# A banded attention with a feed-forward block: another weighing in the scheduler that writes out its order

## The chip, the cores and the metric

The kernel runs on one core of a Trainium2 chip. The metric is the device time of one execution in microseconds (us), taken as the median of three runs. Engines are named as in the profile: PE is TensorE (matrix products), DVE is VectorE, ACT is ScalarE, POOL is GpSimd, and SP is the engine whose queue issues nearly all DMAs.

## The reference

Attention over 4 batches, 8 heads, 768 positions and 64 columns a head, in which a position sees the last `n_local` positions and the first `n_global`, with a slope per head on the distance; then a layer norm and two matrix products with a ReLU between them, added to the attention's output.

```python
def _attn_ref(q, k, v, n_global, n_local):          # q, k, v: 4 x 8 x 768 x 64
    scores = scale * np.matmul(q, k.transpose(0, 1, 3, 2))
    rel = pos[:, None] - pos[None, :]
    is_global = pos[None, :] < int(n_global)         # 8 here
    is_local = (rel >= 0) & (rel < int(n_local))     # 96 here
    dist = np.where(is_global & ~is_local, float(n_local), np.abs(rel))
    slopes = 2.0 ** (-8.0 * (np.arange(H) + 1) / H)  # 1/2, 1/4, ... 1/256
    scores = np.where(is_global | is_local, scores - slopes * dist, -1e9)
    ...                                              # softmax
    return np.matmul(a, v)

def _moe_ref(x, g_ln, w_ch1, w_ch2):                 # x: 4 x 768 x 512
    xn = (x - mu) / np.sqrt(var + 1e-06) * g_ln
    ch = np.maximum(xn @ w_ch1, 0.0) @ w_ch2         # 512 x 2048 and 2048 x 512, float64
    return x + ch
```

## The kernel before, in words

The work is cut into 24 tiles of 128 positions. Tiles 0 to 3 are the first 128 positions of each batch ("short": one block of keys, computed in fp32); tiles 4 to 23 follow batch by batch and see two blocks of keys. Two tiles make a chunk; the products of the feed-forward block run chunk by chunk. Each value that enters a product in the long part is split in two fp16 numbers, an upper and a lower part, and a product takes three matmuls.

**A short tile t** goes through: load of k, q, v; `tk`, `tq` (PE turns k and q with matmuls against `ident`); `km`, `qm` (ACT or DVE copies them from PSUM to SBUF); `S` (PE, scores in tile `s`); `R` (DVE adds the mask, takes the minimum, into `T`); `E` (ACT, exponential); `tp` (PE turns T), `pl` (copy to `pT`); `P` (PE, `pv`); `X`, `B`, `A`, `C` (DVE: division, statistics, spread, centring to `xs`); `W` (POOL, the root of `rs`); `xr` (scaling of `xs`); `tx` (PE turns it), `xh`, `xl` (ACT upper part and DVE lower part, in `xT`).

**The weights** come as 16 pieces of 1 MB in float64; pieces 0 to 7 are of the first matrix, two pieces for four columns of blocks. Of piece n: `wb` brings it (SP); `wr` (ACT, a relu over the low words); `ws`, the sign step (DVE, one bit of 1024 16-bit words); `wz`, sizes (ACT); `ww`, the shift (DVE); `wu`, the upper half, into `w1h` or `w2h` (ACT, POOL or DVE); `wl`, the lower half, into `w1l` or `w2l` (POOL or DVE). A piece is staged in a tile `st`, or, for six of them, in the later home of other halves, so that it is seen in rows as `w2h` or `w2l`.

**The products.** The first product of chunk c has eight steps, tiles `f_c_0`, `f_c_2`, ... `f_c_14`, of 24 matmuls each. Step f needs `xT` of both tiles of the chunk and pieces 2j and 2j+1 with j = f // 4 rounded down, so f_0_0 and f_0_2 need pieces 0 and 1, f_0_4 and f_0_6 pieces 2 and 3, f_0_8 pieces 4 and 5. ACT and DVE make the two halves of `h` from it, which frees its bank of PSUM. The second product follows two chunks (later one) at a time.

**What sets the order.** Each step is entered as a task with its engines, a cost in us, the tasks that it waits for, the buffers that it takes and a rank. `Plan.order` walks a clock of its own through all tasks: of the tasks that can start next on an engine (within 0.05 us) it takes that with the least rank, and for a task that several engines can do it takes the engine that would end it first. The list that comes out is the order in which each engine gets its instructions, and an engine does them in that order. Tasks marked `port` on DVE, and all on POOL, are never planned at the same time. Where PE is planned to have no work in the first 90 us, `blank` puts matmuls of 512 columns whose result nobody reads. Ranks come from the constants at the head of the file (`QUICK`, `PIECE`, `START`). All instructions are issued through one recording helper, and so all carry line 193 in the profile of before (199 after the change); steps are told apart by their tiles.

Of the kernel before, what the change touches and what calls it, by code (L numbers as in the profile page):

```python
# [16 lines left out]
AF = mybir.ActivationFunctionType  # L17
# [7 lines left out]
P = 128  # L25
# [18 lines left out]
CT = 2  # L44
# [6 lines left out]

QUICK = (0.0, -5.2, 7.7, 16.9)
PIECE = (1.8, 5.3, 15.0)
START = 37.6
SIDE = (-1.1, 1.1)
UNTIL = 90.0
# [28 lines left out]
class Plan:  # L85
# [9 lines left out]
    def order(self):  # L95
# [83 lines left out]
def banded(ctx, tc, q, k, v, n_global, n_local, g_ln, w1, w2, out, flag):  # L179
# [98 lines left out]

    def build_mask0(h, engine):
        if engine == "ACT":  # L280
            act.activation(out=mask0[:, h], in_=made["d0"], func=AF.Copy, scale=Z * 2.0 ** -(h + 1))
        else:
            vec.tensor_scalar_mul(out=mask0[:, h], in0=made["d0"], scalar1=Z * 2.0 ** -(h + 1))

# [3 lines left out]

    def build_mask1(h, engine):
        if engine == "ACT":  # L290
            act.activation(out=mask1[:, h], in_=made["d"], func=AF.Copy, scale=Z * 2.0 ** -(h + 1))
        else:
            (vec if engine == "DVE" else pool).tensor_scalar(out=mask1[:, h], in0=made["d"], scalar1=Z * 2.0 ** -(h + 1), scalar2=None, op0=ALU.mult)

    task("starts", "POOL", 1.0, starts, take={"h": ["mask1_7"]})
    task("warm", "ACT", 1.5, warm, ["ident"], rank=-40)
# [4 lines left out]
    task("distance", "DVE", 1.25, distance, ["away"], rank=-1)  # L301
    for n in range(H):
        h = n % 4 * 2 + n // 4
        task(f"mask0_{h}", {"DVE": 0.17, "ACT": 0.35}, 0, lambda engine, h=h: build_mask0(h, engine), ["distance"], rank=0.1 * n)
    task("globals", "DVE", 0.25, globals_first, [f"mask0_{h}" for h in range(H)], rank=30)
    for h in range(H):
        task(f"mask1_{h}", {"POOL": 0.87, "ACT": 0.42, "DVE": 0.3}, 0, lambda engine, h=h: build_mask1(h, engine), ["globals"], rank=45, port=True)
    task("gb", "SP", 0.6, lambda: load.dma_start(out=gb, in_=g_ln.partition_broadcast(P)), rank=9, dma=0.7)
# [7 lines left out]
    def weight(n):  # L316
# [89 lines left out]
    def quick(t, rank):  # L406
# [107 lines left out]
    def tile_(t, ranks, gates):  # L514
# [91 lines left out]
        else:  # L606
# [21 lines left out]
            kready.append("globals")  # L628
            kready += [f"mask1_{h}" for h in range(H)]

        for g in range(ng_):
            rank = ranks[g]
            slow = 1.05 if short else 0.48
            first_take = {"tile": [f"X{t}"]} if g == 0 else {}
            task(f"S{t}_{g}", "PE", slow, lambda g=g: scores(g), kready + ([f"S{t}_{g - 1}"] if g else []) + gates[g], rank=rank - 20, take={"s": [f"R{t}_{g}"], **first_take})
            task(f"R{t}_{g}", "DVE", 0.85, lambda g=g: reduce(g), [f"S{t}_{g}"] + ([f"mask0_{h}" for h in heads(g)] if short else []), rank=rank - 3, take={"T": [f"tp{t}_{g}" if short else f"pl{t}_{g}"]})
            task(f"E{t}_{g}", "ACT", 1.7 if short else 1.2, lambda g=g: exps(g), [f"R{t}_{g}"], rank=rank - 3)
            if short:
                task(f"tp{t}_{g}", "PE", 0.7, lambda g=g: flip(g), [f"E{t}_{g}"], rank=rank - 20, take={"f1" if t < 2 and g == 0 else "f2": [f"pl{t}_{g}"]}, slack=0.8 * (t > 1))
# [86 lines left out]
    def ffn1(c, f, rank):  # L726
# [353 lines left out]
```

## Time and profile before

| | |
|---|---|
| runs | 628.87 us median of 3, 627.67 to 629.8 |
| profiled execution | 629.0 us, of which 627.1 us span |
| granted clock of PE, mean | 0.989 |
| PE busy | 611.4 us (97%), 5337 matmuls |
| DVE, ACT, POOL busy | 404.2, 329.7, 51.5 us |
| DMA | 88.27 MB, mean 141 GB/s |

The span runs from the first instruction to the last; 1.9 us of the execution lie outside it. Busy time of PE holds the blank matmuls too. A row of the timeline gives start, length, engine, line, operation, tiles written and read, and in brackets how long the engine had been idle before it and what it had waited for. An instruction's length can overlap the next one's start; where spacing matters, starts are compared.

### The profile page before, as it was taken

Reading aid. Unit: us, or ns where it says so; the run is one execution under the profiler, and the core shown is the slowest. Engines: PE = TensorE matmul, PEld = TensorE weight load, DVE = VectorE, ACT = ScalarE, POOL = GpSimd, SP = SyncE. Lnnn points to the kernel's source line nnn. Section 1 sums busy time; section 2 is a strip of 40 time slices with the busy share of each in tenths; the row PEclk is TensorE's granted clock in tenths of the full one; section 3 lists DMA queues with packets and bytes.
Section 4 is the critical chain, followed back from the end, with each engine's and each line's share of the span. In section 5 each row is a group of like instructions: output and inputs, shape, how many; then the busy total and the mean of one; then the engine's idle time right before and its main releaser. Section 6 shows DMA issues by size and latency. Waiting matters only on the chain.

```text
span 627.1 us, 13530 instructions
## 1 busy us (share of the span) xinstructions
PE 611.4 (97%) x5337; PEld 434.5 (69%) x5337; DVE 404.2 (64%) x979; ACT 329.7 (53%) x823; POOL 51.5 (8%) x52
## 2 busy tenths in 40 slices
PE   8979999999999999999999999999999999999995
PEld 4857896457957956956966966965965975975852
DVE  5899999985764763764754754754755744646740
ACT  5888998863644643644644544644652634520200
POOL 2210101130100100110100100200100100000000
PEclk9789999999999999999999999999999999999999
DMA  8982999989758757659657568786577653231000
GB/s 225 322 276 75 240 225 230 219 163 231 149 120 184 103 121 172 108 110 220 109 120 163 112 118 174 132 167 148 114 126 140 126 107 81 56 52 42 10 9 30
DMA packets 247304, 88.27 MB, mean 141 GB/s; under 512 B 237377, under 2 KB 237377, under 8 KB 247233
## 3 DMA queue, kind: packets, MB, share of 16 engines
q1 hardware_dynamic: 246944, 87.32, 65.0%
q8 instruction: 44, 0.72, 0.5%
q14 instruction: 28, 0.22, 0.1%
q10 hardware_dynamic: 288, 0.00, 0.0%
HBM read 38.01 MB, written 6.29 MB: 71 GB/s over the span
## 4 chain that ended last, share of the span: by engine, by line
PE 89%; DVE 6%; DMA 1%; issue 1%; ACT 1%; SPq 0%; DVEq 0%; ACTq 0%
PE f L193 77%; PE s L193 6%; PE pv L193 5%; DVE st L193 1%; DVE w2l L193 1%; DMA w2h<-in_moe_w_ch_dram 1%; DVE T L193 1%; DVE h L193 1%; SPq L193 0%; ACT T L193 0%; DVE w2h L193 0%; DVE xT L193 0%; PE tp L193 0%; PE blank L193 0%; DVE x L193 0%
## 5 line engine op out<-in xcount | busy, mean ns | idle before, releaser
L193 PE MATMUL f<-xT,w1h 128*128 128x256 f16 x1536 | 256.5, 273 | 3.9 <-ACT kT L193 2.2
L193 PE MATMUL f<-w2h,h 128*128 128x512 f16 x768 | 237.2, 379 | 0.3 <-DVE h L193 0.3
L193 PE MATMUL f<-xT,w1l 128*128 128x256 f16 x768 | 210.1, 274 | 0.0
L193 PEld LDWEIGHTS <-h 128*128 128x128 f16 x1152 | 110.1, 98 | 123.9 <-issue 0.6
L193 PEld LDWEIGHTS <-w1h 128*128 128x128 f16 x1536 | 148.2, 98 | 21.6 <-DVE xT L193 2.5
L193 PE MATMUL f<-w2l,h 128*128 128x512 f16 x384 | 145.5, 379 | 0.0
L193 ACT ACTIVATE h<-f 128x512 f16<-128x512 f32 x96 | 56.7, 590 | 91.8 <-PE f L193 91.4
L193 DVE TENSOR_TENSOR pn<-T,pn 128x512 f16<-128x512 f32 x79 | 56.0, 709 | 74.6 <-ACT pn L193 74.6
L193 ACT ACTIVATE T<-T,mn 128x256 f32<-128x256 f32 (+1 forms) x192 | 92.4, 482 | 2.9
L193 DVE SCALAR_TENSOR_TENSOR h<-f,h 128x512 f16<-128x512 f32 x96 | 66.0, 687 | 34.1 <-ACT h L193 34.1
L193 ACT ACTIVATE mn<-nm 128x2 f32<-128x2 f32 (+1 forms) x88 | 17.7, 201 | 124.4 <-DVE nm L193 124.4
L193 PEld LDWEIGHTS <-w1l 128*128 128x128 f16 x768 | 75.3, 98 | 9.7 <-issue 0.8
L193 DVE CUSTOM_DVE_ANT_0 T<-s,mask 128x256 f32<-128x256 f32 (+1 forms) x192 | 68.2, 396 | 11.8 <-PE s L193 10.6
L193 POOL TENSOR_TENSOR rs<-rs,half 128x1 f32<-128x1 f32 x24 | 24.9, 1038 | 429.2 <-DVE rs L193 405.2
L193 PE MATMUL s<-kT,qT 128*128 128x128 f16 (+1 forms) x704 | 55.4, 226 | 1.2 <-ACT T L193 1.2
L193 ACT ACTIVATE pn<-T 128x512 f16<-128x512 f32 x80 | 50.1, 626 | 1.6
L193 PEld LDWEIGHTS <-pT 128*128 128x128 f16 x960 | 38.8, 98 | 10.3
L193 DVE SCALAR_TENSOR_TENSOR x<-f,x 128x512 f32<-128x512 f32 x24 | 16.6, 690 | 40.0 <-PE f L193 40.0
L193 PE MATMUL pv<-vn,pT 128*128 128x64 f16 x960 | 41.0, 193 | 0.0
L193 PEld LDWEIGHTS <-qT 128*128 128x128 f16 x640 | 38.7, 98 | 2.9
L193 ACT ACTIVATION_READ_ACCUMULATOR T<-T,mn 128x1 f32 x192 | 35.9, 187 | 0.0
L193 DVE TENSOR_TENSOR x<-pv,r 128x512 f32<-128x512 f32 x24 | 16.6, 691 | 9.5 <-PE pv L193 8.6
(126 smaller groups left out, 459.4 us busy)
## 6 DMA issues: line engine op xcount, KB each, us to landing
st<-in_moe_w_ch_dram SPq DMA_DIRECT2D x10, 1024.0 KB, 6.1
kf<-in_k_dram SPq DMA_DIRECT2D x28, 256.0 KB, 4.1
vf<-in_v_dram SPq DMA_DIRECT2D x28, 256.0 KB, 3.5
qf<-in_q_dram SPq DMA_DIRECT2D x24, 256.0 KB, 4.1
out_dram<-x SPq DMA_DIRECT2D x24, 256.0 KB, 2.6
qT<-qT SPq DMA_DIRECT2D x40, 128.0 KB, 2.5
w2h<-in_moe_w_ch_dram SPq DMA_DIRECT2D x3, 1024.0 KB, 7.4
w2l<-in_moe_w_ch_dram SPq DMA_DIRECT2D x3, 1024.0 KB, 9.1
```

Source lines behind the costliest of these rows:

```text
L193: ins = getattr(self.engine, name)(*args, **kw)
```

## The change

Four things change. The scheduler, in weighing which engine would end a task first, adds to an engine's time the cost of tasks of that engine alone that stand ready with no higher rank (`behind`). The sign step is entered with 1.33 us instead of 0.7 and is no longer marked `port`. The masks are built by DVE alone, that of one head as half or less of another's, instead of one instruction a head on DVE, ACT or POOL. And more ranks are set apart from each other by a new table, `OFFSET`, with all constants given new values; the weights' loads now come 21 ranks ahead of their work instead of 12.

```diff
-QUICK = (0.0, -5.2, 7.7, 16.9)
-PIECE = (1.8, 5.3, 15.0)
-START = 37.6
-SIDE = (-1.1, 1.1)
+QUICK = (0.0, -3.4, 15.7, 13.1)
+PIECE = (-1.3, 6.5, -36.8)
+START = 30.8
+SIDE = (-0.9, -0.5)
+AHEAD = 0.37
+OFFSET = (2.7, 8.2, -16.5, -0.9, -21.0)
...
+        def behind(engine, key):
+            rank = tasks[key][3]
+            return sum(tasks[k][0][engine] for k, t in ready[engine].items() if len(tasks[k][0]) == 1 and tasks[k][3] <= rank and t < engines[engine] + AHEAD)
...
-                        ends = {o: max(ready[o][key], engines[o]) + c + FAVOR.get(o, 0.0) for o, c in costs.items()}
+                        ends = {o: max(ready[o][key], engines[o] + behind(o, key)) + c + FAVOR.get(o, 0.0) for o, c in costs.items()}
...
-    def build_mask0(h, engine):
...
+    def scaled_down(to, of, power):
+        vec.tensor_scalar_mul(out=to, in0=of, scalar1=2.0 ** -power)
+
+    def build_mask0():
+        vec.tensor_scalar_mul(out=mask0[:, 0], in0=made["d0"], scalar1=Z * 0.5)
+        scaled_down(mask0[:, 2], mask0[:, 0], 2)
+        scaled_down(mask0[:, 4:7:2], mask0[:, 0:3:2], 4)
+
+    def build_odd():
+        scaled_down(mask0[:, 1::2], mask0[:, 0::2], 1)
...
+    def build_mask1():
+        vec.tensor_scalar_mul(out=mask1[:, 0], in0=made["d"], scalar1=Z * 0.5)
+        scaled_down(mask1[:, 1], mask1[:, 0], 1)
+        scaled_down(mask1[:, 2:4], mask1[:, 0:2], 2)
+        scaled_down(mask1[:, 4:8], mask1[:, 0:4], 4)
...
-        task(f"wb{n}", "SP", 0.6, bring, before, rank=rank - 12, take={} if n in homes else {"st": [f"wl{n}"]}, dma=3.0)
+        task(f"wb{n}", "SP", 0.6, bring, before, rank=rank + OFFSET[4], take={} if n in homes else {"st": [f"wl{n}"]}, dma=3.0)
...
-        task(f"ws{n}", "DVE", 0.7, signs, [f"wr{n}"], rank=rank, port=True)
+        task(f"ws{n}", "DVE", 1.33, signs, [f"wr{n}"], rank=rank)
...
-            task(f"E{t}_{g}", "ACT", 1.7 if short else 1.2, lambda g=g: exps(g), [f"R{t}_{g}"], rank=rank - 3)
+            task(f"E{t}_{g}", "ACT", 1.7 if short else 1.2, lambda g=g: exps(g), [f"R{t}_{g}"], rank=rank + (OFFSET[0] if short else -3))
...
-        task(f"hl{c}_{f}", "DVE", 0.7, low, [f"hh{c}_{f}"], rank=rank - 6)
+        task(f"hl{c}_{f}", "DVE", 0.7, low, [f"hh{c}_{f}"], rank=rank + (OFFSET[2] if c < 2 else -6))
```

What this does to the order is seen in three places. SP, at the start of the program, where loads are issued: `kf`, `qf`, `vf` are k, q, v of a short tile, and rows with `in_moe_w_ch_dram` are pieces of weights. Before:

```order
L193 DMA kf_0_99<-in_k_dram 128x8x64
L193 DMA qf_0_111<-in_q_dram 128x8x64
L193 DMA vf_0_114<-in_v_dram 128x8x64
L193 DMA w2h<-in_moe_w_ch_dram 128x2x512
L193 DMA kf_0_131<-in_k_dram 128x8x64
L193 DMA qf_0_154<-in_q_dram 128x8x64
L193 DMA vf_0_164<-in_v_dram 128x8x64
L193 DMA w2h<-in_moe_w_ch_dram 128x2x512
```

The same place of SP after the change:

```order
L199 DMA w2h<-in_moe_w_ch_dram 128x2x512 x2
L199 DMA kf_0_113<-in_k_dram 128x8x64
L199 DMA qf_0_115<-in_q_dram 128x8x64
L199 DMA vf_0_129<-in_v_dram 128x8x64
L199 DMA w2l<-in_moe_w_ch_dram 128x2x512
```

Pieces 0 and 1 have moved ahead of all loads of the first tile. On PE, the first turn of k (`tk`) stood behind 7 blank matmuls and now stands behind 41; before f_0_0 there were 57 blanks in all and 14 later, and now there are 77 and none.

ACT, from its first work on the data on; the rows on `w2h` are steps of pieces 0 and 1, the one on `w1h` is the upper half of piece 0, and `kT`, `qT` are copies of what PE has turned. After the change:

```order
L199 ACTIVATE w2h<-w2h,less 128x1024
L199 ACTIVATE d<-rel,hl 128x256
L199 ACTIVATE w2h,big<-w2h 128x1024
L199 ACTIVATE w2h<-w2h,less 128x1024
L199 ACTIVATE kT_0_194<-tk_186 128x512
L199 ACTIVATE w1h<-w2h 128x2x512
L199 ACTIVATE qT_209<-tq_201 128x512
```

Before, `kT`, `d`, `qT` and four masks came first here and piece 0 followed. Now three weight steps lead, and the copy of the turned k stands between the relu of piece 1 and the upper half of piece 0.

POOL, from its first step after the constants on. Before:

```order
L193 TENSOR_SCALAR mask_88<-d 128x256 x2
L193 TENSOR_TENSOR rs<-rs,half 128x1 x2
L193 TENSOR_TENSOR w1h<-w2l,fill 128x2x512
L193 TENSOR_TENSOR rs<-rs,half 128x1
L193 TENSOR_TENSOR w1l<-st_463,w1h 128x2x512
```

After the change, behind the two halves of piece 2 and two roots, the halves of pieces 3, 4 and 5 and the lower half of piece 7:

```order
L199 TENSOR_TENSOR w1h<-w2l,fill 128x2x512
L199 TENSOR_TENSOR w1l<-w2l,w1h 128x2x512
L199 TENSOR_TENSOR w1h<-st_268,fill 128x2x512
L199 TENSOR_TENSOR w1l<-st_268,w1h 128x2x512
L199 TENSOR_TENSOR w1h<-st_305,fill 128x2x512
L199 TENSOR_TENSOR rs<-rs,half 128x1
L199 TENSOR_TENSOR w1l<-st_305,w1h 128x2x512
L199 TENSOR_TENSOR w1l<-w2h,w1h 128x2x512
```

POOL has 17 steps on weights in all, where it had 2, and 35 lower parts of probabilities (`pn`), where it had 1; the roots `rs` stand between them.

## Rows read from the trace of the kernel before

**Rows 1.** The page: busy time of each engine.

```profile
PE 611.4 (97%) x5337; PEld 434.5 (69%) x5337; DVE 404.2 (64%) x979; ACT 329.7 (53%) x823; POOL 51.5 (8%) x52
```

**Rows 2.** Busy time in three stretches; the first row names the columns.

```profile
core 0: us, PE busy (x) PEld busy (x) DVE busy (x) ACT busy (x) POOL busy (x), PEclk, DMA share, GB/s
5.46:40.64 35.18, 30.25 (x185) 21.57 (x183) 31.45 (x102) 30.30 (x87) 9.36 (x5) 0.90 1.00 304
40.64:76.05 35.41, 33.71 (x278) 28.18 (x278) 32.71 (x60) 29.58 (x57) 3.93 (x3) 0.95 0.68 181
76.05:550.00 473.95, 473.54 (x4385) 338.77 (x4383) 305.00 (x760) 259.22 (x661) 36.42 (x33) 1.00 0.72 145
```

**Rows 3.** Timeline of PE: f_0_0 begins, blanks, f_1_0 begins (start, length, what).

```profile
40.77 0.37 PE L193 MATMUL f<-xT,w1h 128*128 128x256 f16 x1 [0.31 <-DVE xT L193]
...
55.40 1.46 PE L193 MATMUL blank<-ident 128*128 128x512 f16 x6
...
76.05 0.67 PE L193 MATMUL f<-xT,w1h 128*128 128x256 f16 x2
```

**Rows 4.** Chain of waits in order of time: start, length, what.

```profile
3.63 6.96 DMA w2h<-in_moe_w_ch_dram
10.67 1.24 ACT w2h L193
...
47.48 2.62 PE f L193 x24
```

**Rows 5.** Instructions of PE by shape, 40.7 to 76.05: busy, mean ns | idle before.

```profile
L193 PE MATMUL f<-xT,w1h 128*128 128x256 f16 x128 | 22.9, 283 | 1.7 <-DVE h L193 1.3 <-DVE xT L193 0.3
...
L193 PE MATMUL pv<-vf,pT 128*128 128x64 f32 x32 | 4.0, 268 | 0.0
L193 PE MATMUL blank<-ident 128*128 128x512 f16 x14 | 3.7, 379 | 0.0
```

**Rows 6.** Two stretches of 2 us, columns as in rows 2.

```profile
18.00:20.00 2.00, 2.00 (x11) 1.80 (x10) 1.97 (x6) 1.97 (x12) 0.00 (x0) 0.50 1.03 420
...
42.00:44.00 2.00, 2.00 (x12) 1.42 (x11) 2.00 (x3) 0.43 (x1) 0.00 (x0) 0.54 0.39 113
```

**Rows 7.** Instructions on the staged pieces `st`: from issue to landing.

```profile
DMA to landing us min/median/max: 5.0/6.1/10.2
```

**Rows 8.** Timeline of PE: its first matmuls.

```profile
1.51 3.17 PE L193 MATMUL blank<-ident 128*128 128x512 f16 x7 [1.51 <-DVE ident L193]
```

**Rows 9.** Timelines of POOL and DVE: steps that met, and one alone.

```profile
25.18 2.40 POOL L193 TENSOR_TENSOR rs<-rs,half 128x1 f32<-128x1 f32 x1 [11.00 <-DVE rs L193]
...
49.60 0.92 POOL L193 TENSOR_TENSOR rs<-rs,half 128x1 f32<-128x1 f32 x1 [11.16 <-DVE rs L193]
...
36.52 1.92 POOL L193 TENSOR_TENSOR w1h<-w2l,fill 128x1024 f16<-128x1024 f32 x1 [4.38 <-issue]
...
64.26 2.46 POOL L193 TENSOR_TENSOR w1l<-st,w1h 128x1024 f16<-128x1024 f32 x1 [13.74 <-ACT w1h L193]
...
24.95 1.36 DVE L193 TENSOR_SCALAR w2h<-w2h 128x1024 uint16<-128x1024 uint16 x1
...
37.16 2.36 DVE L193 SCALAR_TENSOR_TENSOR w2l<-w2l 128x1024 int32<-128x1024 int32 x1
```

**Rows 10.** Instructions of DVE by shape, 5.46 to 40.7.

```profile
L193 DVE CUSTOM_DVE_ANT_0 T<-s,mask 128x128 f32<-128x128 f32 x24 | 5.5, 286 | 1.5 <-PE s L193 1.4 <-issue 0.2
...
L193 DVE TENSOR_SCALAR mask<-d 128x256 bf16<-128x256 f32 x6 | 1.7, 332 | 0.0
...
L193 DVE TENSOR_SCALAR qT<-tq 128x512 f32<-128x512 f32 x1 | 0.7, 677 | 0.0
```

**Rows 11.** The transposes of `pT`: landing, then the tightest one, issue and first use.

```profile
DMA to landing us min/median/max: 3.0/3.2/6.4
...
148.28 1.33 SPq L193 DMA_TRANSPOSE pT<-pn  x1
...
154.07 0.40 PE L193 MATMUL pv<-vn,pT 128*128 128x64 f16 x8
```

More of the change, by code (lines that the diff above doesn't have):

```diff
@@ L287, in globals_first @@
         vec.scalar_tensor_tensor(out=d[:, 0, :GK], in0=made["g"][:, :GK], scalar=made["cnt"][:, 1:2], in1=d[:, 0, :GK], op0=ALU.add, op1=ALU.min)
[L289 to L295, printed above, removed]
+    def build_mask1():
[3 more added lines that the diff above has]
+        scaled_down(mask1[:, 4:8], mask1[:, 0:4], 4)
+    task("starts", "POOL", 1.0, starts, take={"h": ["mask1"]})
     task("warm", "ACT", 1.5, warm, ["ident"], rank=-40)
@@ L301, in banded @@
     task("distance", "DVE", 1.25, distance, ["away"], rank=-1)
[L302 to L307, printed above, removed]
+    task("mask0", "DVE", 0.55, build_mask0, ["distance"], rank=0)
+    task("mask0_odd", "DVE", 0.26, build_odd, ["mask0"], rank=0.1)
+    task("globals", "DVE", 0.25, globals_first, ["mask0"], rank=30, port=True)
+    task("mask1", "DVE", 1.3, build_mask1, ["globals"], rank=45, port=True)
     task("gb", "SP", 0.6, lambda: load.dma_start(out=gb, in_=g_ln.partition_broadcast(P)), rank=9, dma=0.7)
@@ L628, in tile_ @@
             kready.append("globals")
-            kready += [f"mask1_{h}" for h in range(H)]
+            kready.append("mask1")
         for g in range(ng_):
@@ L635, in tile_ @@
             task(f"S{t}_{g}", "PE", slow, lambda g=g: scores(g), kready + ([f"S{t}_{g - 1}"] if g else []) + gates[g], rank=rank - 20, take={"s": [f"R{t}_{g}"], **first_take})
-            task(f"R{t}_{g}", "DVE", 0.85, lambda g=g: reduce(g), [f"S{t}_{g}"] + ([f"mask0_{h}" for h in heads(g)] if short else []), rank=rank - 3, take={"T": [f"tp{t}_{g}" if short else f"pl{t}_{g}"]})
-            task(f"E{t}_{g}", "ACT", 1.7 if short else 1.2, lambda g=g: exps(g), [f"R{t}_{g}"], rank=rank - 3)
+            task(f"R{t}_{g}", "DVE", 0.85, lambda g=g: reduce(g), [f"S{t}_{g}"] + ([("mask0", "mask0_odd")[g]] if short else []), rank=rank + (OFFSET[0] if short else -3), take={"T": [f"tp{t}_{g}" if short else f"pl{t}_{g}"]})
+            task(f"E{t}_{g}", "ACT", 1.7 if short else 1.2, lambda g=g: exps(g), [f"R{t}_{g}"], rank=rank + (OFFSET[0] if short else -3))
             if short:
                 task(f"tp{t}_{g}", "PE", 0.7, lambda g=g: flip(g), [f"E{t}_{g}"], rank=rank - 20, take={"f1" if t < 2 and g == 0 else "f2": [f"pl{t}_{g}"]}, slack=0.8 * (t > 1))
-                task(f"pl{t}_{g}", EITHER, 0, lambda engine, g=g: moved(g, engine), [f"tp{t}_{g}"], rank=rank - 3, take={"pT": [f"P{t}_{g}"]})
+                task(f"pl{t}_{g}", EITHER, 0, lambda engine, g=g: moved(g, engine), [f"tp{t}_{g}"], rank=rank + (OFFSET[0] if short else -3), take={"pT": [f"P{t}_{g}"]})
                 pready = [f"pl{t}_{g}"]
             else:
-                task(f"ph{t}_{g}", {"ACT": 0.64, "DVE": 0.45}, 0, lambda engine, g=g: high(g, engine), [f"E{t}_{g}"], rank=rank - 3, take={"pn": [f"pt{t}_{g}"]}, port=True)
-                task(f"pl{t}_{g}", {"POOL": 1.22, "DVE": 0.7}, 0, lambda engine, g=g: low(g, engine), [f"ph{t}_{g}"], rank=rank - 3, port=True)
+                task(f"ph{t}_{g}", {"ACT": 0.64, "DVE": 0.45}, 0, lambda engine, g=g: high(g, engine), [f"E{t}_{g}"], rank=rank + (OFFSET[0] if short else -3), take={"pn": [f"pt{t}_{g}"]}, port=True)
+                task(f"pl{t}_{g}", {"POOL": 1.22, "DVE": 0.7}, 0, lambda engine, g=g: low(g, engine), [f"ph{t}_{g}"], rank=rank + (OFFSET[0] if short else -3), port=True)
                 task(f"pt{t}_{g}", "SP", 1.35, lambda g=g: across(g), [f"pl{t}_{g}"], rank=rank - 10, take={"pT": [f"P{t}_{g}"]}, dma=1.47)
@@ L704, in normal @@
         c, n_ = divmod(t, CT)
-        task(f"X{t}", "DVE", 1.1, divide, [last], rank=rank - 4, take={"h" if t == 2 * CT + 1 else "x": [f"O{t}"]})
-        task(f"B{t}", "DVE", 0.72, stats, [f"X{t}"], rank=rank - 4)
-        task(f"A{t}", "DVE", 0.3, spread, [f"B{t}"], rank=rank - 4)
+        task(f"X{t}", "DVE", 1.1, divide, [last], rank=rank + (OFFSET[1] if short else -4), take={"h" if t == 2 * CT + 1 else "x": [f"O{t}"]})
+        task(f"B{t}", "DVE", 0.72, stats, [f"X{t}"], rank=rank + (OFFSET[1] if short else -4))
@@ L708, in normal @@
+        task(f"A{t}", "DVE", 0.3, spread, [f"B{t}"], rank=rank + (OFFSET[1] if short else -4))
         task(f"W{t}", "POOL", 0.98, root, [f"A{t}"], rank=rank - 12)
-        task(f"C{t}", "DVE", 0.74, centred, [f"A{t}", "gb"], rank=rank - 4, take={"T": [f"xt{t}" if short else f"xl{t}"]}, port=True)
+        task(f"C{t}", "DVE", 0.74, centred, [f"A{t}", "gb"], rank=rank + (OFFSET[1] if short else -4), take={"T": [f"xt{t}" if short else f"xl{t}"]}, port=True)
         whole = {"xT": [f"F{c}_{NF - 2}"]} if n_ == 0 else {}
@@ L711, in normal @@
         if short:
-            task(f"xr{t}", {"ACT": 0.75, "DVE": 0.7}, 0, scaled, [f"W{t}", f"C{t}"], rank=rank - 4)
+            task(f"xr{t}", {"ACT": 0.75, "DVE": 0.7}, 0, scaled, [f"W{t}", f"C{t}"], rank=rank + (OFFSET[1] if short else -4))
             task(f"xt{t}", "PE", 0.7, flip, [f"xr{t}"], rank=rank - 20, take={"f1" if t < 2 else "f2": [f"xl{t}"]}, slack=1.0 * (t > 1))
-            task(f"xh{t}", "ACT", 0.66, turned_high, [f"xt{t}"], rank=rank - 4, take=whole)
-            task(f"xl{t}", "DVE", 0.72, turned_low, [f"xh{t}"], rank=rank - 4)
-        else:
-            task(f"xh{t}", "ACT", 0.62, high, [f"W{t}", f"C{t}"], rank=rank - 4, take={"pn": [f"xa{t}"]})
-            task(f"xl{t}", "DVE", 0.72, low, [f"xh{t}"], rank=rank - 4, port=True)
+            task(f"xh{t}", "ACT", 0.66, turned_high, [f"xt{t}"], rank=rank + (OFFSET[1] if short else -4), take=whole)
@@ L719, in normal @@
+            task(f"xl{t}", "DVE", 0.72, turned_low, [f"xh{t}"], rank=rank + (OFFSET[1] if short else -4))
+        else:
+            task(f"xh{t}", "ACT", 0.62, high, [f"W{t}", f"C{t}"], rank=rank + (OFFSET[1] if short else -4), take={"pn": [f"xa{t}"]})
+            task(f"xl{t}", "DVE", 0.72, low, [f"xh{t}"], rank=rank + (OFFSET[1] if short else -4), port=True)
             task(f"xa{t}", "SP", 1.35, across, [f"xl{t}"], rank=rank - 12, take=whole, dma=1.47)
@@ L762, in ffn1 @@
         task(key, "PE", 2.62, products, after, rank=rank, take={tag: [f"hl{c}_{f}"]})
-        task(f"hh{c}_{f}", {"ACT": 0.62, "DVE": 0.72}, 0, high, [key], rank=rank - 6, take={"h": last[c:c + 1] if c < 2 else last})
-        task(f"hl{c}_{f}", "DVE", 0.7, low, [f"hh{c}_{f}"], rank=rank - 6)
+        task(f"hh{c}_{f}", {"ACT": 0.62, "DVE": 0.72}, 0, high, [key], rank=rank + (OFFSET[2] if c < 2 else -6), take={"h": last[c:c + 1] if c < 2 else last})
+        task(f"hl{c}_{f}", "DVE", 0.7, low, [f"hh{c}_{f}"], rank=rank + (OFFSET[2] if c < 2 else -6))
         steps.append(key)
```

6 lines of the change are left out of this document (1 added, 5 removed).

## The prediction

> **What bounds the kernel now.** I read the page first: TensorE is busy for 611.4 of 627.1 us [rows 1]. A share that high says that only the places where TensorE does nothing useful can be won, so the second view is the span cut into stretches [rows 2]. From 76.05 us until 550 TensorE is busy for 473.5 of 473.95 us. Before that, VectorE (DVE) and ScalarE (ACT) are as full as TensorE: DVE 31.45 of 35.18 us and then 32.71 of 35.41. So the kernel has a head of 76 us set by DVE and ACT, and a body set by TensorE. Nothing of TensorE's useful work changes, so the change is worth what it takes off the head.
>
> The head splits where the first product starts, at 40.77 us, when TensorE at last has xT from DVE; its eight steps of chunk 0 (PSUM tiles f_0_0 to f_0_14) are over at 76.05, when f_1_0 begins [rows 3]. Those 35.3 us hold 28.6 of useful work: eight steps of 2.62 us [rows 4] are 21.0; the attention matmuls among them (32 of pv as [rows 5] says, 16 of s, 24 that turn a tile) are 7.6 at a start-to-start spacing of about 0.11 us. The other 6.7 us are loss, in four parts: 14 blank matmuls, spaced 0.22 us (six take 1.46 with 0.38 for the last one's own run, [rows 3]), 3.0; waits, 1.3 for DVE's step on h [rows 5] and 0.2 for ACT, together 1.6; the clock, which is down to half (granted 0.54 from 42 to 44, the level of 1.2 GHz, after TensorE had stood waiting for f_0_0) [rows 6], half of the 3.2 us from 40.8 to 44, some 1.5; and 0.6 that I can't place.
>
> **The change, part by part.** The table of offsets moves work, and the order shows how. SP now issues two weight pieces of 1 MB before the first k, q, v. On PE 41 blanks stand before the first turn of k (7 before), and none after f_0_0 has begun (14 before; in all 77 against 71). On POOL stand 17 weight steps in place of 2. The masks are built by DVE alone.
>
> *Up to f_0_0.* The first weight piece is now the first transfer: issued at 0.74, it lands between 0.74 + 5.0 (the least of the staged pieces) and 0.74 + 6.96 (the first piece before, which had three loads ahead of it) [rows 4, 7]. I take 6.2, near the lone piece, since nothing is ahead of it. The next follows 1.05 MB / 420 GB/s [rows 6] = 2.5 us later, and the first k some 0.7 us after that, near 9.5. But the 41 blanks run first: they start at 1.51, at about 0.43 us each (seven take 3.17, [rows 8]) until about 6 us, where the spacing halved before; so some 10.5 are done by 6.0, and 30.5 more at 0.22 end at 12.6. The turn of k is over at 13.1, three us after k lies there. ACT takes the copy of that turn before the upper half of piece 0 (order of ACT), so DVE's lower half of piece 0 waits: relu 6.2 to 7.4 [rows 4], sign step to 8.7, sizes to 10.0, relu of piece 1 to 11.2, ACT idle to 13.1, copy to 13.7, upper to 14.8. DVE, which ended the sign step of piece 1 at 13.4, sits 1.4 us.
>
> DVE's work from 5.46 until the xT that releases f_0_0 was 31.45 us [rows 2]. In the new order the same list has one sign step more (+1.3, [rows 9]); one scaling of xs, as wide as the qT copy (+0.7, [rows 10]); four score reductions less (4 x 5.5/24 = -0.9, [rows 10]); the qT copy and one pT copy of the same width gone to ACT (-1.4); and one shift counted as 2.36, which could go on only when POOL's step beside it ended, at 36.52 + 1.92 = 38.44, and so holds some 1.1 of waiting [rows 9] that I book below. Masks: DVE spent 1.7 on six of 256 columns [rows 10] and some 0.6 on four of half that width. It now makes eight of 128 to 1024 columns, 3072 in all. At the same 0.28 per 256 that is 3.4; halving a bf16 mask isn't in the trace, and if it goes twice as fast, 1.7. I take 2.3, which is near the middle and no change, and keep -0.6 to +1.1; what ACT and POOL save on masks (0.9, 2.7) is off the path. Sum: 31.45 + 1.3 + 0.7 - 0.9 - 1.4 - 1.1 = 30.05. Idle: it was 35.18 - 31.45 = 3.7. Now 0.8 (sign step of piece 0 waits for its relu), the 1.4 above, and four short waits on ACT, whose list up to the second xT I count at about 28 us from 6.2 on, with 1.9 of waiting besides: 0.4 before tile 1's reduction, 0.6 before the sign step of piece 3, 0.5 before tile 1's division, 1.2 before tile 1's scaling; 4.9 in all. One wait for POOL, 1.0. So f_0_0 starts at 5.46 + 30.05 + 4.9 + 1.0 = 41.4, against 40.77: +0.6.
>
> *From f_0_0 to f_1_0.* The useful 28.6 stays. The blanks are gone (-3.0). The clock: TensorE still stands idle a little before f_0_0, so I leave half, 0.8. Waits: POOL now makes the halves of pieces 2 to 5. After the shift of piece 3, which stands just ahead of the last xT, so at 40.7, it has three uppers of 1.92, three lowers of 2.46 - 0.36 = 2.1 and one root of 0.92 to do before f_0_8 may start [rows 9]: 13.0 us. While DVE runs a sign step or a shift, POOL stands: a root that lasts 0.92 alone lasted 2.40 beside two sign steps [rows 9]. Six such DVE steps of 1.15 to 1.2 fall between (7.0), so piece 5 is ready at 60.7. TensorE reaches f_0_8 at 41.4 + 0.8 + 4 x 2.62 + 7.2 = 59.9 (all attention work but one group), so it waits about 0.8 to 1.1. One more wait of 1.2 at f_0_12, whose bank is freed by a DVE step that now stands behind tile 2's division and statistics. Waits 2.3, loss 3.1 against 6.7. f_1_0 starts at 41.4 + 28.6 + 3.1 = 73.1 against 76.05: -3.0.
>
> The Trainium skill, page "SBUF — State Buffer", section "Who interferes with whom", says that a DVE instruction with at most one SBUF input and outside the two-port modes does not contend with GpSimd; the change treats the sign step so. The 2.40 us of the root beside two sign steps speaks against it, so the sum goes by the row; by the rule it would end 1.5 us lower (a rival below).
>
> *The body.* 35 lower parts of the probabilities go to POOL (1 before). POOL takes 1.92 to 2.46 us for 1024 columns [rows 9], so 1.0 to 1.2 for these 512 and up to 1.5 where it meets DVE, which takes 0.7 itself; a transpose starts up to 0.8 later. The tightest of the 80 before was issued at 148.28 and used at 154.07, 5.8 us, of which landing takes 3.2 in the median [rows 11]; the others have more. The cover holds: 0. Uncovered it would be 0.8 for each tight group, 2 to 4 us over the body.
>
> Sum: 627.1 - 3.0 = 624.1 of span, and 1.9 around it as in the profiled run (629.0), gives 626.0. That run lies 0.1 above the median of 628.87, so I forecast **625.9 us**.
>
> **The rivals.** *The head gets all that the order promises.* No blank stands after f_0_0, which means that the scheduler, counting the sign step at its real length for the first time, sees no hole there. If ACT's waits halve (-2.0 at f_0_0) and only 0.6 of loss remains: 39.4 + 28.6 + 0.6 = 68.6, 7.5 off, 621.4 us. Against it: the 41 blanks overrun the landing of k.
> *The sign step leaves POOL alone.* Then POOL's chain is shut out only by shifts (3.5 us, not 7.0), piece 5 is ready at 57.2 and the wait at f_0_8 and half of that for POOL before f_0_0 go: 1.5 off, 624.4 us. By the Trainium skill's rule above it would go this way.
> *The early weights only push the attention back.* If the first piece lands at 7.7, ACT's chain slips 1.5; if the clock falls to half between 15 and 30 us, as it had before by 18 [rows 6], tile 0's and 1's matmuls add another 1.5. f_0_0 at 44.4, and the 3.0 are eaten: 628.9, no change.
> *POOL becomes the bound (slower).* Eight POOL steps lie on the way to f_0_8. If four of them are shut out by two DVE steps in a row instead of one, as the root was, piece 5 is late by 4 x 1.2 = 4.8 more: 630.7. It decides as soon as piece 5 is ready later than about 63 us. For it: POOL's two weight steps before both met DVE (a shift stood 1.1 us). Against: four lowers leave DVE, and it has room.
>
> **How the numbers follow.** Chances: forecast 0.42 (its own range 623.5 to 627.6), all of the head 0.18, the sign step free 0.08, pushed back 0.17, POOL bound 0.15. A measurement of this kernel can tell about 0.3%, 1.9 us, from no change: faster is below 627.0, slower above 630.8. Faster: 0.36 of the forecast + 0.18 + 0.08 = 0.62; the same: 0.06 + 0.14 + 0.03 = 0.23; slower: 0.03 + 0.12 = 0.15. The range takes in the first rival and most of the slow one, with the masks' and the landing's bounds: 621.2 to 630.3.
>
> **What would show it.** Right: f_0_0 within 1.5 us of 41.4; f_1_0 near 73; TensorE's only notable waits between at f_0_8 and f_0_12; the first turn of k right behind the blanks near 12.6, with ACT idle before it; POOL roots and weight steps longer than 0.92 and 2.1 beside sign steps; no wait of TensorE from f_1_0 on. Wrong: f_0_0 past 43, a wait over 3 us at f_0_4 or f_0_8, or waits in the body for pT.

## The result, and the profile after

The changed kernel takes 632.67 us (median of 6 runs, 631.76 to 633.06) where the kernel before took 628.82 in the same job: a ratio of 1.0066, 95% interval 1.0045 to 1.0086. It is slower by some 4 us; forecast were 625.9, with a range to 630.3. The profiled execution took 633.06 us, of which 631.3 are span.

The page's row on the engines answers to [rows 1]:

```profile
PE 613.9 (97%) x5343; PEld 434.4 (69%) x5343; DVE 390.2 (62%) x922; ACT 326.0 (52%) x815; POOL 132.1 (21%) x109
```

DVE lost 14 us of busy time and POOL gained 81. Yet the head did not shrink. The three stretches, cut where f_0_0 and f_1_0 now begin, answer to [rows 2]:

```profile
core 0: us, PE busy (x) PEld busy (x) DVE busy (x) ACT busy (x) POOL busy (x), PEclk, DMA share, GB/s
5.46:42.80 37.34, 34.12 (x205) 22.20 (x204) 32.07 (x97) 30.28 (x77) 8.70 (x5) 0.97 0.99 302
42.80:78.42 35.62, 32.12 (x265) 27.99 (x264) 34.35 (x56) 28.40 (x63) 18.74 (x11) 0.93 0.60 175
78.42:550.00 471.58, 470.13 (x4352) 335.28 (x4350) 286.75 (x708) 253.81 (x648) 101.72 (x83) 1.00 0.72 143
```

f_0_0 starts at 42.80 (before 40.77), f_1_0 at 78.42 (before 76.05). DVE is busier from f_0_0 to f_1_0, 34.35 of 35.62 us, with fewer instructions (56 against 60). TensorE's timeline shows the places that answer to [rows 3, 8]: the first blanks, f_0_0, f_0_10, f_0_12, f_1_0, and the second step of the second product. The bracket gives how long TensorE had been idle and what it had waited for.

```profile
1.52 11.52 PE L199 MATMUL blank<-ident 128*128 128x512 f16 x41 [1.52 <-DVE ident L199]
...
42.80 0.63 PE L199 MATMUL f<-xT,w1h 128*128 128x256 f16 x2
...
65.89 0.39 PE L199 MATMUL f<-xT,w1h 128*128 128x256 f16 x2 [1.10 <-DVE h L199]
...
71.08 0.38 PE L199 MATMUL f<-xT,w1h 128*128 128x256 f16 x2 [2.40 <-DVE h L199]
...
78.42 0.38 PE L199 MATMUL f<-xT,w1h 128*128 128x256 f16 x2
...
104.64 0.39 PE L199 MATMUL f<-w2h,h 128*128 128x512 f16 x1 [1.10 <-DVE h L199]
```

The three waits are all for DVE's step on h. The chain of waits says why h is late at f_0_12 (start, length, what; it answers to [rows 4]):

```profile
65.23 0.60 DVE h L199
65.83 1.78 DVE r L199
67.64 0.21 DVE r L199
67.90 0.04 issue
67.94 0.70 DVE x L199
...
70.43 0.61 DVE h L199
71.04 0.04 issue
71.08 4.45 PE f L199 x24
```

A step on 128x8 numbers, `r<-sm` (the sums of the exponentials, before their reciprocal), takes 1.78 us of the chain; then h is late, and f_0_12 itself takes 4.45 us instead of 2.62. The granted clock (third number from the end) is 0.64 from 72 to 76 us, so TensorE is for most of this at its lower level of 1.2 GHz, right after standing idle:

```profile
72.00:76.00 4.00, 4.00 (x25) 3.13 (x24) 3.53 (x5) 1.66 (x4) 1.42 (x1) 0.64 0.36 82
```

The timelines of DVE and POOL, put side by side in pairs (they answer to [rows 9]), show what the slow steps met:

```profile
32.45 2.15 DVE L199 TENSOR_SCALAR r<-sm 128x8 f32<-128x8 f32 x1
31.50 3.07 POOL L199 TENSOR_TENSOR w1l<-w2l,w1h 128x1024 f16<-128x1024 f32 x1
...
44.73 3.15 DVE L199 SCALAR_TENSOR_TENSOR st<-st 128x1024 int32<-128x1024 int32 x1
43.83 2.97 POOL L199 TENSOR_TENSOR w1l<-w2l,w1h 128x1024 f16<-128x1024 f32 x1
...
56.81 2.45 DVE L199 SCALAR_TENSOR_TENSOR xs<-x,mv,gb 128x512 f32<-128x512 f32 x1
56.57 2.15 POOL L199 TENSOR_TENSOR w1l<-st,w1h 128x1024 f16<-128x1024 f32 x1
...
65.75 1.85 DVE L199 TENSOR_SCALAR r<-sm 128x8 f32<-128x8 f32 x1
65.43 2.15 POOL L199 TENSOR_TENSOR w1l<-w2h,w1h 128x1024 f16<-128x1024 f32 x1 [6.71 <-ACT w1h L199]
...
37.34 1.29 DVE L199 TENSOR_SCALAR st<-st 128x1024 uint16<-128x1024 uint16 x1
36.85 1.82 POOL L199 TENSOR_TENSOR rs<-rs,half 128x1 f32<-128x1 f32 x1 [2.27 <-DVE rs L199]
```

Add start and length: r ends at 34.60 and POOL's subtraction at 34.57; the other r at 67.60 and POOL at 67.58; the shift at 47.88, 1.1 us after POOL's 46.80, which is about its own length (1.2 alone). The `w1l` row of a pair is POOL's subtraction, which makes the lower half of a weight piece. Each of these DVE steps stood until POOL's instruction was over; below this is called a hold. The last pair is the other direction: POOL's root ends at 38.67, the sign step beside it at 38.63. Over 43 to 80 us seven DVE steps took 8.4 us more than the same forms take alone (in the kernel before none did).

The Trainium skill, page "SBUF — State Buffer", section "Who interferes with whom", says that the one of DVE and GpSimd that issues first keeps the shared pair of ports for a whole instruction, and that a DVE step with two SBUF inputs contends with a GpSimd step that reads SBUF. By that the shifts and xs had to stand behind the subtractions, and the rows agree: the shift at 44.73 and xs at 56.81 began after POOL's step and took 3.15 and 2.45 us, where they take 1.2 and 0.74 alone. Of this section the prediction had used only the sentence on steps with one input. It took the sign step to be covered, without asking whether that step falls under the sentence's own exception, the two-port modes.

### The profile page after: what moved, and what is told of

Read it like the earlier page. It is cut to its first block, busy times and chain, and to the rows that moved or that the text cites. A ratio compares the mean times of both kernels' runs of the same rounds, so it can differ in the third digit from the quotient of the medians.

```text
span 631.3 us, 13587 instructions
## 1 busy us (share of the span) xinstructions
PE 613.9 (97%) x5343; PEld 434.4 (69%) x5343; DVE 390.2 (62%) x922; ACT 326.0 (52%) x815; POOL 132.1 (21%) x109
## 4 chain that ended last, share of the span: by engine, by line
PE 86%; DVE 5%; ACT 4%; SPq 2%; DMA 1%; issue 1%; POOL 1%; DVEq 0%; ACTq 0%; POOLq 0%
PE f L199 74%; PE s L199 6%; PE pv L199 5%; SPq L199 2%; DVE st L199 1%; DMA w2l<-in_moe_w_ch_dram 1%; ACT T L199 1%; ACT st L199 1%; POOL rs L199 1%; DVE xs L199 1%; ACT h L199 1%; DVE h L199 1%; DVE r L199 0%; DVE x L199 0%; POOL w1l L199 0%
## 5 line engine op out<-in xcount | busy, mean ns | idle before, releaser
L199 DVE TENSOR_TENSOR pn<-T,pn 128x512 f16<-128x512 f32 x45 | 31.7, 705 | 80.0 <-ACT pn L199 80.0
L199 POOL TENSOR_TENSOR pn<-T,pn 128x512 f16<-128x512 f32 x35 | 43.3, 1237 | 99.5 <-ACT pn L199 65.6
L199 POOL TENSOR_TENSOR kn<-kf,kn 128x512 f16<-128x512 f32 x23 | 28.5, 1239 | 164.1 <-ACT kn L199 127.7
L199 PE MATMUL s<-kT,qT 128*128 128x128 f16 (+1 forms) x704 | 56.8, 225 | 1.2 <-ACT qT L199 0.9
L199 POOL TENSOR_TENSOR rs<-rs,half 128x1 f32<-128x1 f32 x24 | 21.8, 908 | 132.1 <-DVE rs L199 131.7
```

The lines of the kernel that those rows point to most:

```text
L199: ins = getattr(self.engine, name)(*args, **kw)
```

## The experiments

Theory A: POOL's steps on weights shut DVE out, so h is late. Theory B: the early weight pieces push the attention back and the products follow. The ratio of each run is to the kernel before in the same job, with the 95% interval behind it. Medians of the kernel before in the jobs below are 627.8 to 628.1 us.

**POOL's subtraction replaced.**

```diff
         def lower(engine):
-            (pool if engine == "POOL" else vec).tensor_tensor(out=dl, in0=staged[n][3], in1=dh, op=ALU.subtract)
+            pool.memset(dl, 0.0) if engine == "POOL" else vec.tensor_tensor(out=dl, in0=staged[n][3], in1=dh, op=ALU.subtract)
```

> The kernel after, in the same order on every engine, but the 11 lower halves of weights that POOL makes are replaced by a POOL memset of the same tile (their values are left out). Theory A (POOL's steps on weights shut DVE out, so that h comes late and TensorE waits at f_0_10 and f_0_12): DVE's time above nominal from 43 to 80 us falls from 8.4 us to under 3, both waits (1.1 and 2.4) go, the clock stays up, f_1_0 starts near 75 instead of 78.4: 628 to 629 us. Theory B (the two early weight pieces push the attention back, and the products follow): f_0_0 stays at 42.8, f_1_0 stays past 77.5, time 631.5 to 633.

Measured: 623.15 us, ratio to before 0.9933 (0.9913 to 0.9954); f_0_0 at 40.05, f_1_0 at 70.62. B falls: the two early pieces still lead, and f_0_0 comes 2.75 us sooner. More time is won than A expected, yet A's own number is missed: DVE's time above nominal from 43 to 80 us falls from 8.4 only to 4.9 us, not to under 3. The edit changes three things at once: the memset reads nothing, it takes 0.95 us alone instead of 2.15, and it need not wait for the upper half. In timelines of DVE and POOL of this run:

```profile
53.38 0.74 DVE L199 SCALAR_TENSOR_TENSOR xs<-x,mv,gb 128x512 f32<-128x512 f32 x1
54.03 2.10 DVE L199 TENSOR_SCALAR w2h<-w2h 128x1024 uint16<-128x1024 uint16 x1
53.12 1.83 POOL L199 MEMSET w1l<- 128x1024 f16 x2
```

Beside the memsets xs takes 0.74, as alone, not 2.45. But the sign step at 54.03 ends at 56.13, 1.2 us after POOL's 54.95, which is about its own length (1.3 alone): a memset holds it too.

> As the run with POOL's lower halves as a memset (values of the 11 lower halves left out), but each memset is issued twice, so that POOL is busy some 2.0 to 2.3 us a piece, as long as the subtraction alone (2.1), and the pieces are ready no sooner. If theory A holds (the subtraction shuts DVE out; a memset does not), the time stays within 1 us of the single memset, 623 to 624. If what counted was only that POOL was done sooner, it goes back towards the kernel after: 629 to 632.

Each memset was issued twice. Measured: 622.52 us, 0.9914 (0.9893 to 0.9936). So POOL's time on a piece hardly matters. But each of the two instructions still takes 0.95 us, and the sign step above shows that a memset does not leave DVE alone, as was expected of it. Whether a hold is cheap here because nothing is read or because it is short, these two runs don't tell. The next ones keep the values and all waits for data.

**Is the small step the main victim?**

```diff
-            vec.tensor_scalar(out=r, in0=sm, scalar1=PS * 1e-9, scalar2=1.0 if short else VS, op0=ALU.add, op1=ALU.mult)
-            vec.reciprocal(out=r, in_=r)
+            vec.reciprocal(out=r, in_=sm)
...
+                vec.scalar_tensor_tensor(out=x, in0=sums.pop(t), scalar=1.0 / VS, in1=r.unsqueeze(2).to_broadcast([P, H, D]), op0=ALU.mult, op1=ALU.mult)
```

> The kernel after without one DVE instruction a tile: the 128x8 step r<-sm (it adds 4.1e-6 to sums of exponentials and scales them) goes; the reciprocal reads the sums themselves, and the scale of 1/256 of the long tiles is taken into the product that follows. All other work stands in the same order. In the kernel after this step lasted 0.16 us alone, but 2.15, 1.26 and 1.85 us beside POOL's subtractions, 4.8 us too much before f_1_0, and the last two stand ahead of the waits at f_0_10 and f_0_12. Theory A with this step as the main victim: the waits at f_0_10 and f_0_12 (3.5) and the half clock behind them (1.8) mostly go, f_1_0 at 74 to 75.5: 628 to 629.5. If the stall only moves to the next step that POOL shuts out (a shift, xs): less than 1.5 us gained, 631.5 to 633.

Measured: 628.56 us, 1.0012 (0.9997 to 1.0027): 4.1 us back (3.4 by the ratios) from an instruction of 0.16 us. f_0_12 starts at 67.94, after a wait of 0.50. DVE's loss to holds up to 80 us hardly changes, 10.4 us before the edit and 10.1 now, so what counts is where a hold falls, and r stands ahead of the h that TensorE waits for. The reciprocal, which now reads the sums in place of r<-sm, meets the same subtraction and is not held; the sign step is (DVE, then POOL, twice):

```profile
64.51 0.19 DVE L199 RECIPROCAL r<-sm 128x8 f32<-128x8 f32 x1
64.21 2.16 POOL L199 TENSOR_TENSOR w1l<-w2h,w1h 128x1024 f16<-128x1024 f32 x1 [6.72 <-ACT w1h L199]
...
30.60 3.33 DVE L199 TENSOR_SCALAR w2l<-w2l 128x1024 uint16<-128x1024 uint16 x1 [0.41 <-ACT w2l L199]
30.57 2.15 POOL L199 TENSOR_TENSOR w1l<-w2l,w1h 128x1024 f16<-128x1024 f32 x1
```

The sign step ends 1.2 us after POOL's 32.72, so it too is shut out, though the change plans it as free.

> The kernel before without the step r<-sm (reciprocal reads the sums, scale taken into the product). In the kernel before this step lasts 0.2 us in each of the four short tiles and met no POOL step. Theory A: 0.8 us less on DVE before f_1_0 at most, time 0 to 0.9 us below before's. If the step costs by itself (a stop in DVE's pipeline, a semaphore): 2 to 4 us below before.

The same edit on the kernel before: 626.46 us, 0.9979 (0.9960 to 0.9998), 1.6 us less. That is above the 0.9 that I had given for the step alone, but the interval, 0.1 to 2.5 us, takes 0.9 in. So most of the 4.1 comes by POOL's presence, and how much of the rest is the step's own cost stays open. The expectation is wrong in one point. In the kernel before r did meet POOL once, beside the subtraction at 64.26 of [rows 9], and was not held:

```profile
64.52 0.18 DVE L193 TENSOR_SCALAR r<-sm 128x8 f32<-128x8 f32 x1
```

**How long does a hold last?** POOL's 17 steps on weights in two instructions each:

```diff
-            (pool if engine == "POOL" else vec).tensor_tensor(out=dl, in0=staged[n][3], in1=dh, op=ALU.subtract)
+            [pool.tensor_tensor(out=dl[:, :, u:u + 256], in0=staged[n][3][:, :, u:u + 256], in1=dh[:, :, u:u + 256], op=ALU.subtract) for u in range(0, 512, 256)] if engine == "POOL" else vec.tensor_tensor(out=dl, in0=staged[n][3], in1=dh, op=ALU.subtract)
```

(and likewise for the upper half).

> The kernel after with POOL's 17 steps on weights cut into two instructions each, r<-sm kept. If holds last until the running instruction ends: r<-sm is held 1.1 us at most instead of 2.15, f_0_12 starts about 2 us sooner than 71.08, time 630 to 631.5. If the loss goes with POOL's work: 632.5 to 634.

Measured: 628.41 us, 0.9997 (0.9978 to 1.0016), 4.3 below the kernel after and better than expected. r lasts at most 1.15 us, and ends at 33.64 with POOL's first half (33.60), not with its second (34.75). In DVE's timeline, in place of the 2.15 at 32.45:

```profile
32.49 1.15 DVE L199 TENSOR_SCALAR r<-sm 128x8 f32<-128x8 f32 x1
```

The edit together with the one before:

> The kernel after without the step r<-sm, and with each of POOL's 17 steps on weights cut into two instructions of half the columns; the order is the same. In the run without r<-sm alone DVE still lost 10.1 us in single steps up to 80 us (a sign step 3.33 for 1.31, a shift 3.17 for 1.22, xs 2.47 for 0.70). If a DVE step is held until the running POOL instruction ends: no hold over about 1.2 us, DVE's loss up to 80 us halves to about 5, time 626 to 627.5 against 628.56. If loss goes with POOL's whole work, or each half costs POOL a new start: no gain, 628 to 630.

Measured: 626.14 us, 0.9972 (0.9954 to 0.9989), 0.3% below the kernel before. But that kernel without its r step takes 626.46, so the change still wins nothing that can be told from noise. The shift that took 3.15 us in the kernel after, in DVE's timeline:

```profile
43.77 2.19 DVE L199 SCALAR_TENSOR_TENSOR st<-st 128x1024 int32<-128x1024 int32 x1
```

No step of DVE loses over 1.05 us up to 80 us (2.0 before POOL's steps were halved), so a hold lasts until the running instruction ends. But there are more holds, and the sum went only from 10.1 to 8.7 us, not to the 5 that I expected.

**Giving the work back to DVE.** Three runs take work off POOL through the scheduler: `SIDE` for POOL 1.1 instead of -0.5; the same without blanks late in the head; and the sign step marked `port` again.

```diff
-SIDE = (-0.9, -0.5)
+SIDE = (-0.9, 1.1)
```

> The kernel after with one number changed, SIDE for POOL 1.1 as before instead of -0.5, so that the scheduler gives POOL 2 steps on weights instead of 17 and 2 of pn instead of 35. DVE does them itself. Theory A: the stalls of DVE go, it gets 9 lower halves of 1.2 us more, blanks return (32 after f_0_0); waits and half clock at f_0_10 and f_0_12 go: 628 to 630. Theory B: f_0_0 stays near 42.8 and the time near 632 to 633.

Measured: 631.65 us, 1.0049 (1.0027 to 1.0070). DVE's holds are gone (none of over 0.2 us before 130 us), and nearly nothing is won. The profiled execution is the slowest of seven (628.91 to 634.06) and holds a wait of 1.91 for the DMA of xT at 152 us, so it is read only up to there. TensorE's timeline, and DVE's:

```profile
66.49 6.21 PE L199 MATMUL blank<-ident 128*128 128x512 f16 x28
72.53 0.38 PE L199 MATMUL f<-xT,w1h 128*128 128x256 f16 x2
...
71.95 1.23 DVE L199 TENSOR_TENSOR w1l<-w2h,w1h 128x1024 f16<-128x1024 f32 x1
```

f_0_12 starts behind 28 blanks, while piece 7's lower half is done at 73.2. Which of the two delays it?

```diff
-UNTIL = 90.0
+UNTIL = 40.0
```

> The kernel after with SIDE for POOL 1.1 (nearly no work for POOL), and without its 33 blanks from just ahead of f_0_0 on. In that kernel 28 blanks lie before f_0_12, 66.5 to 72.7 us, and the lower half of piece 7 is done at 73.2. Theory A in a wider form (DVE's list sets the head; what POOL does not do DVE has to, and piece 7 comes late): f_0_12 waits for piece 7 about as long, time within 1 us of 631.7, or slower by the clock. Rival (the blanks themselves are the delay): f_0_12 at 67, time 626.

Measured: 631.69 us, 1.0058 (1.0037 to 1.0078). In TensorE's waits the blanks' place is taken by DVE's steps on the weights:

```profile
66.92 0.39 PE L199 MATMUL f<-xT,w1h 128*128 128x256 f16 x2 [1.68 <-DVE w1h L199]
68.19 0.38 PE L199 MATMUL f<-xT,w1l 128*128 128x256 f16 x1 [0.87 <-DVE w1l L199]
70.64 0.61 PE L199 MATMUL f<-xT,w1h 128*128 128x256 f16 x2 [1.44 <-DVE w1h L199]
71.91 0.39 PE L199 MATMUL f<-xT,w1l 128*128 128x256 f16 x1 [0.65 <-DVE w1l L199]
```

f_1_0 starts at 77.81 (77.83 with blanks). So with these ranks DVE sets the head, by its own steps here and by POOL's holds in the kernel after.

```diff
-        task(f"ws{n}", "DVE", 1.33, signs, [f"wr{n}"], rank=rank)
+        task(f"ws{n}", "DVE", 1.33, signs, [f"wr{n}"], rank=rank, port=True)
```

> The kernel after with the sign step marked port again (at 1.33 us), so that it is planned beside no POOL step; POOL then gets 8 steps on weights instead of 17 and 30 of pn, and 41 blanks stand after f_0_0. If the sign step left free was the fault: 629 or less. Theory A, wide form (what POOL gives up DVE must do, and DVE's list sets the head): piece 7 comes late, f_0_12 at 71 to 73, time 631 to 633.

Measured: 634.52 us, 1.0104 (1.0083 to 1.0126), worse than either expectation. f_0_0 comes at 39.36, but f_0_12 at 71.61 behind 27 blanks and piece 7; f_1_0 leads the kernel after by 1.1 us, and the lead is gone at f_2_0 (152.04, after a wait of 0.72 for xT).

**Blanks in the kernel before**, from just ahead of f_0_0 on (`UNTIL = 36.0`):

> The kernel before without the 22 blank matmuls planned from just ahead of f_0_0 on (14 of them behind f_0_0's start); the order of all other work on every engine is the same. My prediction took those 14 blanks for 3.0 us of loss that goes when they go. If so: f_1_0 3 us sooner, 625. If they only stand where TensorE waits for DVE in any case: waits of the same length take their place, f_1_0 within 0.5 of 76.05 and the time within 1 us of before, or up to 2 us slower where the clock falls for lack of work.

Measured: 630.12 us, 1.0035 (1.0020 to 1.0050). Where six blanks stood at 55.40 [rows 3], TensorE now waits, and from 55 to 70 us the granted clock falls from 1.00 to 0.77:

```profile
56.65 0.66 PE L193 MATMUL tp<-ident,T 128*128 128x128 f32 x4 [1.74 <-ACT pT L193]
...
55.00:70.00 15.00, 12.57 (x87) 10.27 (x88) 13.92 (x20) 11.85 (x20) 3.00 (x2) 0.77 0.84 234
```

The blanks were no loss: they lay in waits, and with them the clock stayed up. Up to f_0_0 the order of the two kernels is the same, yet TensorE's first matmul on f comes at 39.02 here and at 40.18 in the kernel before: single executions differ by some 1 us in the place of a step, so smaller differences between runs are not read.

**The early start.** The counts `n_global` and `n_local` fetched by SP ahead of the weights:

```diff
-        made["asked"] = counts(const, act, n_global, n_local)
+        return
...
+    made["asked"] = counts(const, sp, n_global, n_local)
     for fn in plan.order():
```

> The kernel after, but n_global and n_local are fetched by SP's queue ahead of the first two weight pieces instead of by ACT's queue beside them; the rest is in the same order. In the kernel after DVE's first work waits until 8.04 us (5.46 before the change) for these few bytes. Theory B (what comes early pushes the attention back): DVE starts near 5.5, f_0_0 comes 1 to 2 us sooner than 42.8, and the time is 631 to 632. If DVE's list before f_0_0 is held elsewhere (pieces 0 and 1, POOL): f_0_0 within 0.5 of 42.8, time 632 to 633.5, no change.

Measured: 632.77 us, 1.0081 (1.0057 to 1.0104), no change; f_0_0 at 42.69. DVE gains 2.1 us at the start and waits them out before the first sign step:

```profile
5.91 0.17 DVE L199 CAST nf<-nn 128x4 f32<-128x4 int32 x1 [4.44 <-DMA nn<-in_n_local_dram]
...
9.93 1.32 DVE L199 TENSOR_SCALAR w2h<-w2h 128x1024 uint16<-128x1024 uint16 x1 [2.57 <-ACT w2h L199]
```

> Both edits together: no step r<-sm, and the counts fetched first. If they add up, 627 to 628.5, as the kernel before or a little faster. If the second is covered, as the first alone, 628 to 629.5.

Measured: 629.05 us, 1.0017 (1.0002 to 1.0032), as the edit on r alone.

**The body.** The 35 steps on `pn` that POOL makes, as a memset:

```diff
+            (parts.pop(g), pool.memset(pn[:, :, 1, :], 0.0)) if engine == "POOL" else vec.tensor_tensor(out=pn[:, :, 1, :], in0=parts.pop(g), in1=pn[:, :, 0, :], op=ALU.subtract)
```

> The kernel after in the same order, but the 35 lower parts of probabilities (pn) that POOL makes are a POOL memset (their values left out). Theory A for the body (these steps shut DVE out between 80 and 560 us, 20 us of stalls against 5 before, of which only a little reaches TensorE): the 1.1 us wait of the second product near 104.6 goes or not, 1 to 1.5 us less, 631 to 632. If the body's slack covers them, no change: 632.2 to 633.2. If they were most of the loss, 629.

Measured: 634.37 us, 1.0111 (1.0085 to 1.0137). DVE's loss from 130 to 560 us falls from 11.3 to 4.8 us and nothing is won: the body's slack covers it. Why it is rather slower than the kernel after (a wait of 2.05 instead of 1.10 in the second product) stays open.

**The change by halves.** All ranks, `SIDE` and `OFFSET` of before, the other three parts kept (first); the new ranks, `SIDE` and `OFFSET` alone on the kernel before (second):

> The kernel after with all ranks, SIDE and OFFSET as before; kept are the masks by halving, the sign step at 1.33 without port, and the look at work that stands ready. Three lower halves of weights remain on POOL, none of pn. Theory A: nearly no stalls, 627 to 629. Theory B: k, q, v come first again, f_0_0 back at 40.8 or sooner, 627 to 629. If it stays above 631, the ranks are not the cause and one of the other three parts is.

> The kernel before with the new ranks, SIDE and OFFSET alone (old masks, sign step 0.7 with port, no look at ready work). POOL has 8 steps on weights and 29 of pn. Theory A: DVE stalls of some 8/17 of the changed kernel's, 4 us, f_1_0 near 77: 630 to 632. Theory B: pieces 0 and 1 lead as in the kernel after, f_0_0 at 42.8 and the time as after, 632 to 633. If it is at 629 or below, the ranks alone cost nothing.

Measured: 629.48 us, 1.0036 (1.0018 to 1.0053), and 635.71 us, 1.0133 (1.0109 to 1.0158); the second lies above what either theory expected. The ranks (with `SIDE` and `OFFSET`) make the kernel slow; the other parts cost some 2 us alone, but with the new ranks they win 3 to 4 back (635.71 against 632.67, 1.0133 against 1.0066). With the ranks alone f_0_0 is on time (40.29), which B did not expect, and DVE loses only 1.7 us to holds from 43 to 80, less than A expected; piece 7's lower half ends at 73.61 (69.26 before), and f_1_0 starts at 79.46. From 80 to 130 us DVE loses 9.4 us there (8.5 in the kernel after, 2.3 before). So I take it that the new ranks cost by the late piece where DVE makes it, and by holds where POOL does. Which of the ranks' numbers does it was not tried.

## Why the prediction was wrong

- **Up to f_0_0:** forecast 41.4, measured 42.80. DVE was busy for 32.07 us where 30.05 were forecast, and the excess is r at 32.45, held for 2.0. It stood idle for 5.27 us where 5.9 were forecast, but in other places: 2.58 at the start, for the counts `n_global` and `n_local` that now come behind two weight pieces, which the sum put at nothing; 0.18 ahead of the lower half of piece 0 (forecast 1.4); 0.08 for POOL (forecast 1.0). That these nearly cancel is luck. The first turn of k came behind the blanks as forecast (12.88; 12.6), and the masks cost DVE 2.2 (2.3).
- **The step that failed** is "While DVE runs a sign step or a shift, POOL stands", and with it "Waits 2.3, loss 3.1 against 6.7". POOL did stand beside sign steps (the pair at 37.34), but I let DVE shut POOL out and never POOL DVE; from the shift of 2.36 in [rows 9], which showed just that, I even took 1.1 us off DVE's list as gone. Measured is a loss of 35.62 - 28.6 = 7.0: waits 3.5 (none at f_0_8, 1.10 at f_0_10, 2.40 at f_0_12), 1.8 of low clock in f_0_12, 0.6 in f_0_0's step (3.24), 1.1 that I can't place. With the memset, which holds DVE for less, the same order has 70.62 - 40.05 - 28.6 = 2.0 of loss: most of the loss goes with POOL's subtractions, not with the order itself.
- **Blanks, -3.0:** their going was no gain by itself; without them the kernel before is slower.
- **POOL as the bound:** the rival's sign was right and its mechanism not. Pieces 4 and 5 were ready at 58.72, ahead of f_0_8 at 62.01. The rival in which the sign step leaves POOL alone fell with the pair at 37.34. The one in which early weights push the attention back (B) fell with the memset, where f_0_0 comes at 40.05 behind the same early weights; fetching the counts first won nothing either. The range is said to take in most of the slow rival, but it ends at 630.3, below that rival's 630.7.
- **The body:** forecast 0, measured +1.2 (steps stand 2.4 later at f_1_0, 3.6 at the end), by the wait of 1.10 for h at 104.64. No transpose of pT came late, as forecast.

In sum 1.4 + 3.9 + 1.2 on top of 625.9 is 632.4, against 632.67 measured.

## What to carry to other kernels

Work given to POOL is not all taken off DVE: price each POOL step by what DVE needs while it runs, down to its smallest instruction, since a 0.16 us step here lost up to 2.0 us to one. Where such a step stands ahead of the one that frees a PSUM bank, give it a form that doesn't wait (here the reciprocal alone), or cut POOL's instruction in two. And before counting idle-time fillers as loss, ask what the engine would have waited for without them.

## What the runs showed of the hardware

Whether a DVE step was held hung on its form, not on its size. Up to 80 us of all runs, the 68 steps on x and h that read PSUM and met one of POOL's subtractions on weights took 0.69 us in the mean, none over 0.73. The step r<-sm met one 20 times: 12 were held and lost 1.0 to 2.0 us, and 8 took 0.34 at most. What spares those, as the one at 64.52 in the kernel before, stays open. The reciprocal of the same 128x8 numbers met one 8 times and never took over 0.21.

POOL's form counts too. In the runs with POOL's subtraction replaced, the shift at 76.16 (double memset) took 1.21 us and xs at 53.38 (single) took 0.74, as alone, although a memset ran beside each; but the sign step was held by a memset (2.10 at 54.03), and held one in turn (2.14 us at 41.35 with the double memset, 0.95 alone).
